# Another table of steps for a transformer block's early x passes, weight sums and h rounds, and two chunks' fold products ahead of the first transposes

## The chip, the cores and the metric

One core of one Trainium2 chip runs the whole program. The metric is device time in microseconds: the median over several executions. Below, TensorE is PE in the profile's rows (PEld its weight loads), VectorE is DVE, ScalarE is ACT, GpSimd is POOL, and SP is the engine that issues most of the DMAs, in order, from one queue.

## The reference

One block of a transformer in float32, 2048 rows of width 1024, 32 heads of 32, and an inner width of 3584:

```python
qkv = layernorm(x) @ wqkv
pq, pk = q @ w_phi, k @ w_phi                    # per head, 32 x 32
phi_q = concat(softmax(pq), softmax(-pq))        # the same for phi_k
kv, z = phi_k^T @ v, sum_s(phi_k)
o = (phi_q @ kv) / (phi_q @ z + 1e-6)
h = x + o @ wo
out = h + relu(layernorm(h) @ w1) @ w2
```

## The kernel before

**Numbers.** Every float32 product is made of three fast ones. Each operand is split in a high part (a copy in the fast format, made by ACT) and a low part (the rest, made by DVE or POOL). `mm3` (lines 181 to 183) issues high x high, high x low and low x high as three matmuls of 128 x 512. Three such matmuls are one *step* of the program; almost all of TensorE's work is a row of steps.

**Items and steps.** The work is a list of items in an order written out by hand: first q, k and v products by tiles of 128 rows ("kv" and "q" items, 8 steps each, item n begins at step 8n), then attention and `wo`, then the two layers of the MLP, up (from step `up0`, 4 steps an item) and down. `when(step, f, ...)` hangs a piece of side work behind a step; the engines' queues are filled in that order and each engine works through its own in order. So the step numbers decide what stands ahead of what on ACT, DVE, POOL and in SP's queue, not when it runs.

**Weights.** `Units` loads weight chunks into six buffers `raw` on SP's queue (lines 376 to 389), ACT (line 124) and DVE or POOL (line 128) split them into ten buffers `w`, at most 10 steps before their use or paced out further ahead.

**Folds.** `w_phi` is multiplied into the weights of k and q first. The first slab (p = 0) does it at the start: `first_fold(k)` makes the products of chunks k and k + 1 from `wt` (line 324), `first_high` (ACT, line 453) and `first_low` (DVE, line 457) split them. The other seven slabs do it at steps during the kv items: `wt_load(p)` on SP (line 320), `fold_part(p)` (line 335 on TensorE), DVE's transposes (line 355), and a store on SP (line 363); the products come back as `raw` chunks. The slabs p = 4 and 5 fold at steps 140 and 172, and their `wt` is requested at steps 120 and 152.

**x.** Tiles 0 to 7 are normalised and turned by TensorE just before use (`X_STEPS`: load, statistics, power, normalisation, two transposes). Tiles 8 to 15 are normalised early and stored to `xnd` in device memory (`X_EARLY`: load, statistics, normalisation; the store of four DMAs follows 4 steps after), and loaded again much later. All loads of x, and two of these reloads, share two buffers `xin`. DVE makes the statistics (line 221), POOL the power (lines 230 to 232), ACT the normalisation (lines 244 and 251).

**Weight sums.** The MLP saves one product in eight by a scheme of seven products in place of eight, for which sums of blocks of w1 and w2 are made: a set is a load of 512 KB `b` (SP, line 410; in the up stage by ACT's queue), four subtractions on POOL (line 420) and a store `t` (SP, line 423). There are 56 sets, placed by the list `places`, 21 of them ("far") during the first kv items.

**h.** Of h's two halves of rows, the second is normalised and turned in four rounds during the up stage of the first half (`turn_pair`, with DVE's transposes at line 876), and each round ends in seven stores `hs` (`turn_store`, line 900). `h_load` (line 916) brings the seven combinations back as `hT`, `h_high` (ACT, line 924) and `h_low` (DVE, line 928) split them.

Of the kernel before, what the change touches and what calls it, by code (L numbers as in the profile page):

```python
# [25 lines left out]
NP = NC // 2  # L26
# [113 lines left out]
def kernel(  # L140
# [25 lines left out]
    def tp_bank():  # L166
        return psum.tile([P, 512], F32, name="tp", bufs=2)
# [20 lines left out]
    def do(n, k, f, *args):  # L188
        at[n, k].append((f, args))
# [21 lines left out]
    def ln_load(key, parts):  # L211
        xin[key] = lnp.tile([P, D], F32, name="xin")
        n = D // len(parts)
        for j, p in enumerate(parts):
            sp.dma_start(xin[key][:, j * n:(j + 1) * n], p)
# [106 lines left out]
    def fold_mm(p, k, ps, sides=(0, 1)):  # L322
        for i in sides:
            pe.matmul(ps[:, i * P:(i + 1) * P], wt_of[p, i][:, k * P:(k + 1) * P],
                      bd[:, i, :], start=True, stop=True)
# [111 lines left out]
    def first_part(k):  # L437

        g, c = k // 2, k % 2
        if g not in first_ps:  # L440
            first_ps[g] = (ac_bank, mm_bank)[g // 2]()
        return first_ps[g][:, 256 * c:256 * (c + 1)]

    def first_place(k):

        key = ("kv", 0, 0, k)
        if key not in W.split:
            W.places[key] = W.ring.take()
            W.split[key] = W.places[key][1]
        return W.split[key]  # L450

    def first_high(k):
        act.activation(first_place(k)[:, 0, 0:256], first_part(k), AF.Copy)
# [8 lines left out]
    def value_low(k, eng):  # L462
        w = first_place(k)
        raw, place = first_raw.pop(k)
        eng.tensor_tensor(out=w[:, 1, 256:512], in0=raw, in1=f32(w[:, 0, 256:512]), op=ALU.subtract)
        place[0] = k % 2 == 1

    def first_fold(k):
        for i in range(2):
            fold_mm(0, k + i, first_part(k + i))  # L470
# [566 lines left out]
    def item(gen, *args, keys):  # L1037
        items.append((gen, args + (keys,)))
        steps.extend((k,) for k in keys)
        return len(items) - 1  # L1040
# [11 lines left out]
    for b, tiles in enumerate(groups):  # L1052
        for hf in range(2):

            pairs = b == 0 and hf == 0
            for j in range(0, 4, 2 if pairs else 1):
# [3 lines left out]
                for half in range(2):  # L1060
                    n = item(wo_pair, tiles[j:j + 2], hf, half, keys=[("wo", hf, 4 * half + k // 2) for k in range(8)])
# [18 lines left out]
    def x_part(t):  # L1080
        return [x[t * P:(t + 1) * P, :]]
# [6 lines left out]
    def when(step, f, *args):  # L1088

        if step < 8 * first_up:  # L1090
            do(step // 8, step % 8, f, *args)
        else:
            do(first_up + (step - 8 * first_up) // 4, step % 4, f, *args)


    X_STEPS = {1: (None, None, None, None, 5, 7), 2: (None, 6, 8, 10, 12, 13), 3: (None, 10, 11, 14, 18, 20),
               4: (9, 19, 20, 24, 27, 28), 5: (15, 25, 26, 29, 35, 38), 6: (25, 33, 35, 37, 41, 44)}
    X_EARLY = ((48, 74, 86), (64, 84, 98), (88, 102, 112), (100, 115, 138), (116, 140, 154), (142, 158, 170),
               (158, 174, 203), (174, 204, 218))
    for t in range(1, NT):  # L1100
        n = t - 1 if t < HT else q_n[1, t - HT] + 1
        turn = 8 * n + 1
# [2 lines left out]
        else:  # L1105

            load_, stats, norm = X_EARLY[t - HT]
            when(load_, ln_load, ("s", t), x_part(t))
# [22 lines left out]
    for p, n in zip(range(1, 8), (3, 9, 13, 17, 21, 25, 29)):  # L1131
        step = 8 * n + (4 if p > 1 else 7)
# [82 lines left out]
    for u in range(32):  # L1215
        start = 8 * (a0 + u) if u >= 8 else 8 * (last_kv + 4) + 19 * u // 2
        slack = 6 if u < 5 else 0
        if u % 2:
            places = (-8 if u < 12 else -1, 6, 10, 13, 16, 19, 25 if u < 16 else 23)
            when(start + 30 + slack, at_num, u - 1)  # L1220
            when(start + 32 + slack, at_low, u - 1)
        elif u < 16:
            places = (-8 if u < 12 else -1, 6, 10, 13, 16, 19, 25)
        else:
            places = (6, 12, 17, 19, 21, 23, 29)
# [28 lines left out]
    up0 = 8 * first_up  # L1254
    for i in range(4):
        for stage in (0, 1, 2, 3, 9, 4, 5, 6, 7, 8):
            when(wo0 + 64 + 40 * i + LN2[i % 2][stage], ln_pair, 0, i, stage)
        for step, *what in TURNS:
            when(up0 + 25 + 84 * i + step, turn_pair, i, *what)
        for j in range(7):  # L1260
            when(wo0 + 64 + 40 * i + LN2[i % 2][10] + j // 2, ln_store, 0, i, j)
            when(up0 + 25 + 84 * i + 56 + j, turn_store, i, j)
    assert wo_n[8, 0] + 10 < first_up

    def up_step(b, p, m):

        return up0 + 4 * (up_n[b, p, m] + 1 - first_up)

    for j, m in enumerate(UP):

        for g in range(2):
            step = up0 + (8 * j + (-62, -32)[g] if j < 4 else 6 * (j - 4) + 10 + 2 * g)
            high = up0 + (8 * j + (-48, -19)[g] if j < 4 else 6 * (j - 4) + 20 + 2 * g)
            when(step, h_load, 0, m, g)
            when(high, h_high, m, g)
            when(high + (2 if j < 4 else 5), h_low, m, g)
            step = up_step(0, NP - 1, m) + 3 * j
            when(step + 3 * g, h_load, 1, m, g)
            when(step + 18 + 4 * g, h_high, m, g)
            when(step + 21 + 4 * g, h_low, m, g)  # L1280
# [8 lines left out]


    sets = [(w, p, j) for w in (1, 2) for p in range(NP) for j in range(2)]
    places = [64 * q + step for q in range(4) for step in (-9, -1, 7, 15, 23, 31) if 64 * q + step > 9]
    far_sets = len(places)
    places += [264, 274, 284, 294, 314, 364, 374]
    slabs = [8 * kv_n[1, q, HT] for q in range(4)]
    places += sorted([slab + step for slab in slabs for step in (8, 20, 32)] + [slab - 3 for slab in slabs[1:3]])
    places += [up0 + 440 + 25 * n for n in range(14)]
    for n, (step, (w, p, j)) in enumerate(zip(places, sets, strict=True)):
        far = n < far_sets
        when(step, t_load, w, p, j, lnp if step > up0 else fp if far and n % 4 > 1 else tsp)  # L1300
# [4 lines left out]
    for b in range(2):  # L1305
        for m in DOWN:
            n = down_n[b, m, NP - 1] + 1
# [50 lines left out]
    x_open(0)  # L1358
    ln_load(("x", 2), x_part(2))
    turned = []  # L1360
    for j in range(2):
        pt = tp_bank().rearrange("p (k n) -> p k n", k=4)
        for k in range(4):
            pe.transpose(pt[:, k, :], xnt["x", 0][:, (4 * j + k) * P:(4 * j + k + 1) * P], ident)
        act.activation(xT[0][:, 0, 4 * j:4 * j + 4, :], pt, AF.Copy)
        turned.append(pt)
# [3 lines left out]
        both = xT[0][:, :, 4 * j:4 * j + 4, :]  # L1370
        v.tensor_sub(both[:, 1], turned[j], f32(both[:, 0]))

    first_fold(0)
    for k in range(2):
        value_high(k, v.tensor_copy)
    for k in range(2):
        value_low(k, pool)
        first_high(k)
    for k in range(2):
        first_low(k)  # L1380
    first_fold(2)
# [90 lines left out]
```

## Time and profile before

| | us |
|---|---|
| median of 3 executions | 1879.9 (1879.06 to 1880.86) |
| the profiled execution | 1880.66 |
| its span, first to last instruction | 1878.9 |
| TensorE busy | 1861.3 |
| VectorE busy | 1074.5 |
| GpSimd busy | 996.0 |
| ScalarE busy | 747.1 |

The mean granted clock of TensorE is 0.998. A row of a timeline gives the start, the duration, the engine, the line, the operation, what it writes and reads, and how often; in brackets stands the idle time before it and what ended that. A matmul's row is longer than its place in the stream, since the next begins before it ends: the distance from one start to the next, 0.227 us when nothing is missing, is what counts.

### The profile page before, as it was taken

To read this page: it belongs to the slowest core of one execution; us is meant where nothing else is said; L and a number is where in the kernel's file an instruction comes from. 1 tells how busy PE (TensorE), PEld (TensorE's weight loads), DVE (VectorE), ACT (ScalarE), POOL (GpSimd) and SP (SyncE) were. 2 spreads that over 40 slices of the span, in tenths; PEclk is the share of its full clock that TensorE was granted. 3 is DMA by queue.
4 is the path that set the end of the run, shared out by engine and by line. 5 is a ranking of instruction groups with operands and counts; after the bars stand their busy time and mean duration, and the time that the engine had idled before them with its cause. 6 is when DMAs were issued, how large, how long until landed. Compare 5 with 4: busy or idle time off the path is not lost.

```text
span 1878.9 us, 31761 instructions
## 1 busy us (share of the span) xinstructions
PE 1861.3 (99%) x11502; PEld 1527.8 (81%) x11502; DVE 1074.5 (57%) x1714; ACT 747.1 (40%) x1272; POOL 996.0 (53%) x956
## 2 busy tenths in 40 slices
PE   9999999999999999999999999999999999999999
PEld 7777888888887888888888878888888888888887
DVE  7877789677889676465554674444433333343333
ACT  5443334222233122355454554444444444444442
POOL 4767756678745888233332334435444444444443
PEclk9999999999999999999999999999999999999999
DMA  6799877445465666898687997877877677767775
GB/s 215 245 308 327 291 243 241 131 149 175 135 224 184 206 213 215 266 292 294 214 286 247 297 316 240 264 249 259 274 237 216 205 227 240 236 215 219 216 214 178
DMA packets 320492, 441.64 MB, mean 235 GB/s; under 512 B 28112, under 2 KB 182736, under 8 KB 320336
## 3 DMA queue, kind: packets, MB, share of 16 engines
q1 hardware_dynamic: 291168, 398.69, 66.4%
q10 hardware_dynamic: 29168, 40.93, 6.6%
q8 instruction: 90, 1.47, 0.3%
q14 instruction: 66, 0.54, 0.1%
HBM read 297.96 MB, written 141.57 MB: 234 GB/s over the span
## 4 chain that ended last, share of the span: by engine, by line
PE 88%; DMA 5%; DVE 2%; SPq 1%; issue 1%; ACT 1%; POOL 1%; DVEq 0%; ACTq 0%; POOLq 0%
PE mm L181 22%; PE mm L182 22%; PE mm L183 22%; PE ac L183 3%; PE ac L182 3%; PE ac L181 3%; PE tp L181 2%; PE tp L183 2%; PE tp L182 2%; DMA hT<-hs 1%; PE tp L720 1%; PE ac L533 1%; PE ac L720 1%; DMA raw<-in_w_dram 1%; PE tp L288 1%
## 5 line engine op out<-in xcount | busy, mean ns | idle before, releaser
L128 POOL TENSOR_TENSOR w<-raw,w 128x512 fp32r<-128x512 f32 x353 | 476.5, 1352 | 641.7 <-ACT w L124 619.6
L124 ACT ACTIVATE w<-raw 128x512 fp32r<-128x512 f32 x686 | 408.9, 626 | 485.0 <-PE mm L183 221.1
L128 DVE TENSOR_TENSOR w<-raw,w 128x512 fp32r<-128x512 f32 x333 | 279.4, 840 | 508.8 <-ACT w L124 503.0
L181 PE MATMUL mm<-w,xT 128*128 128x512 f32 x752 | 298.3, 397 | 2.9 <-ACT w L124 2.9
L182 PE MATMUL mm<-w,xT 128*128 128x512 f32 x752 | 293.4, 390 | 0.5 <-POOL w L128 0.2
L183 PE MATMUL mm<-w,xT 128*128 128x512 f32 x752 | 292.8, 389 | 0.0
L182 PE MATMUL mm<-hT,w 128*128 128x512 f32 x672 | 261.8, 390 | 2.8 <-DVE hT L928 2.8
L181 PE MATMUL mm<-hT,w 128*128 128x512 f32 x672 | 261.6, 389 | 0.7 <-DVE c L954 0.7
L183 PE MATMUL mm<-hT,w 128*128 128x512 f32 x672 | 261.4, 389 | 0.0
L420 POOL TENSOR_TENSOR b<-b 128x256 f32<-128x256 f32 x168 | 133.4, 794 | 78.5 <-DMA b<-in_w_dram 70.0
L181 PEld LDWEIGHTS mm<-w,xT 128*128 128x128 f32 x752 | 141.3, 188 | 35.1 <-ACT w L124 3.3
L182 PEld LDWEIGHTS mm<-w,xT 128*128 128x128 f32 x752 | 141.4, 188 | 31.0 <-POOL w L128 1.1
L183 PEld LDWEIGHTS mm<-w,xT 128*128 128x128 f32 x752 | 141.3, 188 | 29.8
L181 PE MATMUL mm<-w 128*128 128x512 f32 x392 | 152.5, 389 | 0.0
L182 PE MATMUL mm<-w 128*128 128x512 f32 x392 | 152.5, 389 | 0.0
L183 PE MATMUL mm<-w 128*128 128x512 f32 x392 | 152.5, 389 | 0.0
L182 PEld LDWEIGHTS mm<-hT,w 128*128 128x128 f32 x672 | 126.1, 188 | 30.2 <-DVE hT L928 4.1
L181 PEld LDWEIGHTS mm<-hT,w 128*128 128x128 f32 x672 | 126.1, 188 | 27.4 <-DVE c L954 1.1
L183 PEld LDWEIGHTS mm<-hT,w 128*128 128x128 f32 x672 | 126.2, 188 | 25.9
L522 POOL TENSOR_TENSOR zacc<-zacc,kphi 128x512 f32<-128x512 f32 x60 | 82.7, 1378 | 7.0 <-DVE kphi L514 7.0
L181 PEld LDWEIGHTS mm<-w 128*128 128x128 f32 x392 | 73.6, 188 | 15.3
L183 PEld LDWEIGHTS mm<-w 128*128 128x128 f32 x392 | 73.6, 188 | 15.3
(200 smaller groups left out, 3181.0 us busy)
## 6 DMA issues: line engine op xcount, KB each, us to landing
raw<-t SPq DMA_DIRECT2D x224, 256.0 KB, 4.3
raw<-ad SPq DMA_DIRECT2D x196, 256.0 KB, 3.0
raw<-in_w_dram SPq DMA_DIRECT2D x168, 256.0 KB, 3.4
ad<-c SPq DMA_DIRECT2D x112, 256.0 KB, 4.2
b<-in_w_dram SPq DMA_DIRECT2D x42, 512.0 KB, 5.6
t<-b SPq DMA_DIRECT2D x42, 512.0 KB, 3.9
ad<-s SPq DMA_DIRECT2D x84, 256.0 KB, 4.7
ed<-qe ACTq DMA_DIRECT2D x32, 512.0 KB, 4.3
```

The costliest lines, as they stand in the source:

```text
L124: nc.scalar.activation(w[:, 0, :], raw[1], AF.Copy)
L128: eng.tensor_tensor(out=w[:, 1, :], in0=raw[1], in1=w[:, 0, :].bitcast(F32), op=ALU.subtract)
L181: pe.matmul(ps, a_hi, b_hi, start=first, stop=False, skip_group_check=more)
L182: pe.matmul(ps, a_hi, b_lo, start=False, stop=False, skip_group_check=more)
L183: pe.matmul(ps, a_lo, b_hi, start=False, stop=last, skip_group_check=more)
L288: pe.transpose(pt[:, k, :], xn[:, (4 * j + k) * P:(4 * j + k + 1) * P], ident)
L420: pool.tensor_tensor(out=tsum[j, *out], in0=tsum[j, *a], in1=tsum[j, *b], op=ALU.subtract)
L522: pool.tensor_tensor(out=zacc[s], in0=zacc[s], in1=phi_of[key], op=ALU.add)
L533: pe.matmul(kv_ps[s][g][32 * i:32 * (i + 1), 0:64], vt[:, 32 * h:32 * (h + 1)], phi[:, 64 * h:64 * (h + 1)], start=first, stop=last)
L720: pe.matmul(banks[g][32 * c:32 * (c + 1), r * P:(r + 1) * P], kvL[rows, 4 * q + 2 * sd + h // 4, 32 * (h % 4):32 * (h % 4 + 1)], phT[rows, ...
```

## The change

It has five parts. The products of fold chunks 0 and 1 and their high parts are placed ahead of the transposes of the first x tile. Tile 6's statistics, power and normalisation go 3, 2 and 1 steps earlier. The passes of x tiles 12 to 15 go from load steps 116, 142, 158, 174 to 140, 168, 206, 232, with their statistics 14 steps after each. Of the far sets of weight sums two, at steps 119 and 183, are taken out, and the up stage gets 16 sets at a pace of 22 steps in place of 14 at 25. Of h's rounds, the second half's turns come every 80 steps and not 84; the loads of its combinations are planned up to 3 steps earlier; and the low halves of the first half's last three combinations 2 steps earlier.

```diff
-    X_STEPS = {... 6: (25, 33, 35, 37, 41, 44)}
-    X_EARLY = (... (100, 115, 138), (116, 140, 154), (142, 158, 170),
-               (158, 174, 203), (174, 204, 218))
+    X_STEPS = {... 6: (25, 30, 33, 36, 41, 44)}
+    X_EARLY = (... (100, 115, 138), (140, 154, 166), (168, 182, 203),
+               (206, 220, 230), (232, 246, 268))
...
-            when(up0 + 25 + 84 * i + step, turn_pair, i, *what)
+            when(up0 + 25 + 80 * i + step, turn_pair, i, *what)
...
-            when(up0 + 25 + 84 * i + 56 + j, turn_store, i, j)
+            when(up0 + 25 + 80 * i + 56 + j, turn_store, i, j)
...
-            when(high + (2 if j < 4 else 5), h_low, m, g)
-            step = up_step(0, NP - 1, m) + 3 * j
+            when(high + (2 if j < 4 else 3), h_low, m, g)
+            step = up_step(0, NP - 1, m) + 5 * j // 2
             when(step + 3 * g, h_load, 1, m, g)
...
-    places = [64 * q + step for q in range(4) for step in (-9, -1, 7, 15, 23, 31) if 64 * q + step > 9]
+    places = [64 * q + step for q in range(4) for step in (-9, -1, 7, 15, 23, 31) if 64 * q + step not in (-9, -1, 7, 119, 183)]
...
-    places += [up0 + 440 + 25 * n for n in range(14)]
+    places += [up0 + 440 + 22 * n for n in range(16)]
...
     turned = []
+    first_fold(0)
+    for k in range(2):
+        first_high(k)
     for j in range(2):
         pt = tp_bank().rearrange("p (k n) -> p k n", k=4)
...
-    first_fold(0)
     for k in range(2):
         value_high(k, v.tensor_copy)
     for k in range(2):
         value_low(k, pool)
-        first_high(k)
```

On TensorE, at the start (`ones` is a warm-up, `ident,xn` the transposes of x tile 0, `bd,wt` the fold products, `w,xT` the first projection), old rows with - and new ones with +:

```order
 L1345 MATMUL tp<-ones 128x128 x11
-L1364 MATMUL tp<-ident,xn 128x128 x8
-L324 MATMUL ac<-bd,wt 128x128 x8
+L324 MATMUL ac<-bd,wt 128x128 x4
+L1367 MATMUL tp<-ident,xn 128x128 x8
+L324 MATMUL ac<-bd,wt 128x128 x4
 L583 MATMUL mm<-w,xT 128x512 x4
 L324 MATMUL mm<-bd,wt 128x128 x8
```

Four of the eight products (two rows each in the profile) stand ahead of the transposes now, and four behind.

In SP's queue, near step 116 (`raw<-wpk` and `raw<-in_wv` are halves of one weight chunk, `xnd<-xn` the store of an early x tile, `xin` the load of tile 12, `b` a set's load, `wt` and `wpk<-wp` a fold's weights and result), before:

```order
L376 DMA raw<-wpk_76 128x256
L377 DMA raw<-in_wv_dram 128x256
L258 DMA xnd_102<-xn 32x4x256 x4
L215 DMA xin<-in_x_dram 128x1024
L376 DMA raw<-wpk_76 128x256
L377 DMA raw<-in_wv_dram 128x256
L410 DMA b<-in_w_dram 128x4x256
L320 DMA wt<-in_wqkT_dram 128x1024 x2
L363 DMA wpk_77<-wp 128x4x256 x2
```

and now:

```order
L376 DMA raw<-wpk_76 128x256
L377 DMA raw<-in_wv_dram 128x256
L258 DMA xnd_102<-xn 32x4x256 x4
L376 DMA raw<-wpk_76 128x256
L377 DMA raw<-in_wv_dram 128x256
L320 DMA wt<-in_wqkT_dram 128x1024 x2
L363 DMA wpk_77<-wp 128x4x256 x2
```

Tile 12's load and one set's load have left this place; the slab's last chunk follows the store directly.

On VectorE, at the begin of the up stage (`w<-raw` a weight split, `hT7` the two low halves of one combination, `c` a sum of two banks), before:

```order
L128 TENSOR_TENSOR w_9528<-raw_9383,w_9528 128x512
L128 TENSOR_TENSOR w_9572<-raw_9427,w_9572 128x512
L128 TENSOR_TENSOR w_9618<-raw_9469,w_9618 128x512
L928 TENSOR_TENSOR hT7_9488<-hT7_9488 128x4x256 x2
L954 TENSOR_TENSOR c110_9515<-ac_9623,c110_9515 128x512
```

and now:

```order
L128 TENSOR_TENSOR w_9514<-raw_9369,w_9514 128x512
L128 TENSOR_TENSOR w_9558<-raw_9413,w_9558 128x512
L928 TENSOR_TENSOR hT7_9474<-hT7_9474 128x4x256
L128 TENSOR_TENSOR w_9605<-raw_9455,w_9605 128x512
L928 TENSOR_TENSOR hT7_9474<-hT7_9474 128x4x256
L954 TENSOR_TENSOR c110_9501<-ac_9610,c110_9501 128x512
```

One low half has moved ahead of the third weight split.

More of the change, by code (lines that the diff above doesn't have):

```diff
@@ L1096 @@
     X_STEPS = {1: (None, None, None, None, 5, 7), 2: (None, 6, 8, 10, 12, 13), 3: (None, 10, 11, 14, 18, 20),
-               4: (9, 19, 20, 24, 27, 28), 5: (15, 25, 26, 29, 35, 38), 6: (25, 33, 35, 37, 41, 44)}
-    X_EARLY = ((48, 74, 86), (64, 84, 98), (88, 102, 112), (100, 115, 138), (116, 140, 154), (142, 158, 170),
-               (158, 174, 203), (174, 204, 218))
+               4: (9, 19, 20, 24, 27, 28), 5: (15, 25, 26, 29, 35, 38), 6: (25, 30, 33, 36, 41, 44)}
+    X_EARLY = ((48, 74, 86), (64, 84, 98), (88, 102, 112), (100, 115, 138), (140, 154, 166), (168, 182, 203),
+               (206, 220, 230), (232, 246, 268))
     for t in range(1, NT):
```

## The prediction, made before the changed kernel ran

> **What bounds the kernel now.** I read the page's busy table first, then TensorE's list of waits, then its busy time in stretches of 20 us, and last the instructions around each hole.
>
> ```profile
> span 1878.9 us, 31761 instructions
> PE 1861.3 (99%) x11502; PEld 1527.8 (81%) x11502; DVE 1074.5 (57%) x1714; ACT 747.1 (40%) x1272; POOL 996.0 (53%) x956
> ```
>
> TensorE is the bound: it idles 17.6 us in all. The change moves work and removes none from TensorE, so it can only win holes in TensorE's stream, or open new ones. Where the holes are (waits of PE; then stretch, length, PE busy, granted clock, DMA share, GB/s):
>
> ```profile
> PE mm L181 <- ACT w L124: 2.9, 1, 2.9
> PE mm L182 <- DVE hT L928: 2.8, 3, 1.3
> PE tp L335 <- DMA wt<-in_wqkT_dram: 2.5, 2, 2.3
> ...
> 120.00:140.00 20.00, 16.89 (x190) 1.00 0.96 303
> 140.00:160.00 20.00, 17.46 (x158) 0.96 0.99 324
> 160.00:180.00 20.00, 19.72 (x126) 0.95 0.93 317
> 1060.00:1080.00 20.00, 19.33 (x85) 1.00 1.05 341
> 1100.00:1120.00 20.00, 17.88 (x78) 1.00 0.91 286
> ```
>
> Every large hole lies in a stretch where the DMA engines are full (0.91 to 1.05). There the queue on SP runs late, and TensorE waits for a weight chunk, a fold's weights or a piece of h. All three edits of the step tables touch these stretches. One program step is three matmuls, 0.68 us at the steady 0.227 us from one start to the next.
>
> **The change part by part.**
>
> *a. Fold products first.* The start, in order:
>
> ```profile
> 7.80 1.47 PE L1364 MATMUL tp<-ident,xn 128*128 128x128 f32 x8 [1.91 <-ACT xn L238]
> 8.15 0.49 DVE L460 CAST w<-raw 128x256 fp32r<-128x256 f32 x2 [0.67 <-DMA raw<-in_wv_dram]
> 9.06 3.25 PE L324 MATMUL ac<-bd,wt 128*128 128x128 f32 x16
> 12.07 1.17 PE L583 MATMUL mm<-w,xT 128*128 128x512 f32 x4
> ...
> 8.37:11.78 3.41, 3.41 (x18) 3.41 (x17) 0.35 (x3) 1.96 (x5) 1.41 (x2) 0.50 1.07 373
> ```
>
> The 16 products run from 9.06 to about 12.0 because the granted clock is 0.50 between 8.37 and 11.78. Half of them (8 rows) now stand before the transposes. Their weights `wt` are issued on SP just ahead of the `raw` chunk that lands by 8.15, so 8.15 is their latest; I put them at about 7.5; 8 rows at full clock are 8 x 0.107 = 0.85 us, so the transposes start near 8.3 instead of 7.8. The transposes then run at half clock, then 8 products x 0.213 = 1.7 us, and the first projection starts near 11.4 instead of 12.07. Some of its four matmuls still fall into the slow window. I take -0.5 us; ends: +0.4 (weights only at 8.15, nothing regained) and -2.0 (no slow window).
>
> The Trainium skill, page "TensorE: Matmul & The Clock Gate", Part 1, says that the clock is set by a free-running window of about 3.4 us and halves after an idle one. The trace agrees in length (0.50 for 3.41 us); by that rule real matmuls ahead of 8.37 could keep the next window at full rate, which is rival 2.
>
> *b. Statistics of x tile 6 at step 30.*
>
> ```profile
> 41.99 1.44 DVE L355 STREAM_TRANSPOSE wp<-mm 128x256 f32<-128x256 f32 x4
> 45.98 1.27 DVE L221 BATCH_NORM_STATS2 st<-xin 128x6 f32<-128x512 f32 x2
> 50.30 0.66 PE L288 MATMUL tp<-ident,xn 128*128 128x128 f32 x4 [0.40 <-ACT xn L244]
> ```
>
> They now stand before the eight `wp` transposes and not behind them. The normalisation then waits for the Exp ahead of it on ACT instead, which comes 1.3 us later (near 47.5 to 48.1); normalised by 49.4, the tile is there when TensorE comes at 49.74. The hole at 50.30 (start to start 0.79 against 0.23) closes: -0.55; ends -0.55 and +1.0 (DVE's kv work is now 1.3 us later).
>
> *c. Early x passes and two weight-sum sets out of the crowd.* The first large hole, as PE's rows, the chain that ended there, and SP's queue:
>
> ```profile
> 122.19 0.39 PE L183 MATMUL mm<-w,xT 128*128 128x512 f32 x1
> 125.47 0.50 PE L181 MATMUL mm<-w,xT 128*128 128x512 f32 x1 [2.88 <-ACT w L124]
> 126.19 0.50 PE L182 MATMUL mm<-w,xT 128*128 128x512 f32 x1 [0.22 <-DVE w L128]
> ...
> 119.55 5.14 DMA raw<-in_wv_dram
> ...
> 118.58 0.39 SPq L215 DMA_DIRECT2D xin<-in_x_dram  x1
> ...
> DMA to landing us min/median/max: 2.3/3.5/6.4
> ```
>
> The hole is 3.05 + 0.50 = 3.55 us. The last chunk of `raw` was issued right behind tile 12's 512 KB load and took 5.14 us. That load goes (step 116 to 140). The chunk is issued about 0.3 us sooner and should land in 2.3 to 3.5 us: 1.9 to 3.1 us sooner. I take -2.5; ends -1.0 and -3.5.
>
> The second hole is fold 5 (step 172) against fold 4 (step 140):
>
> ```profile
> 129.99 0.39 PE L183 MATMUL mm<-w,xT 128*128 128x512 f32 x1
> 132.77 0.50 PE L181 MATMUL mm<-w,xT 128*128 128x512 f32 x1
> ...
> 154.43 0.39 PE L183 MATMUL mm<-w,xT 128*128 128x512 f32 x1
> 157.16 0.41 PE L335 MATMUL tp<-wt,wphi 32*32 32x256 f32 x2 [2.34 <-DMA wt<-in_wqkT_dram]
> 161.20 0.80 PE L181 MATMUL mm<-w,xT 128*128 128x512 f32 x1
> ...
> 149.75 0.98 SPq L320 DMA_DIRECT2D wt<-in_wqkT_dram  x2
> SPq L423 <- POOL b L420: 17.0, 8, 4.7
> DMA packets 18136, 20.57 MB, mean 316 GB/s; under 512 B 1205, under 2 KB 17106, under 8 KB 18130
> ```
>
> One passage takes 2.78 us, the other 6.77: 3.99 lost, 2.5 of it idle and the rest mostly the half clock after it. `wt` was planned 20 steps ahead of this fold, so at 154.4 - 13.6 = 140.8, and issued at 149.75. Ahead of it now go tile 12's load and the set of step 119 (its load, its store, and four POOL sums; SP waited 17.0 us for such sums): three times 0.52 MB, which at 316 GB/s is 5.0 us. Tile 12's new load takes the place of tile 13's old one, so that is even. TensorE itself arrives 0.5 + 0.55 + 2.5 = 3.55 us sooner, so of 3.55 + 2.5 us needed 5.0 are there: 1.1 us stay. -2.9; ends 0 and -4.0. The idle in 160 to 180 (0.28 us) should go as well: -0.3, ends 0 and -0.6.
>
> What moves lands in 125 to 235 us: loads of tiles 13, 14, 15 at steps 168, 206, 232 with their stores (four DMAs each) and POOL scales. Each load now has 14 steps, 9.5 us, until DVE wants it. Landing alone takes 6.3 us here, and DVE already lost 1.7 us to one such load:
>
> ```profile
> xin<-in_x_dram SPq DMA_DIRECT2D x4, 512.0 KB, 6.3
>   DVE st L221: 1.7, 1
> ```
>
> DVE's kv steps and half the weight splits queue behind it. Also, the reload of tile 9 (step 257) now shares a buffer with tile 15, whose normalisation stands at step 268, so SP stops some 9 us there. Behind it are chunks wanted at step 320, 50 steps later, and a set whose sums then hold POOL; I find nobody who needs POOL sooner, so nothing. For new waits of DVE and for the two sets that now come in the up stage (16 at a pace of 22 steps, 14 at 25 before) I put +1.0; ends 0 and +5.
>
> *d. h's rounds.* First the low halves at `high + 3`, then the turns of the second half at a pace of 80:
>
> ```profile
> 822.21 1.06 ACT L924 ACTIVATE hT<-hT 128x1024 fp32r<-128x1024 f32 x1 [2.02 <-DMA hT<-hs]
> 824.43 2.35 DVE L928 TENSOR_TENSOR hT<-hT 128x1024 fp32r<-128x1024 f32 x2
> 826.84 0.50 PE L182 MATMUL mm<-hT,w 128*128 128x512 f32 x1 [0.70 <-DVE hT L928]
> ...
> 1040.83 0.90 SPq L900 DMA_DIRECT2D hs<-s  x2
> 1052.47 0.67 SPq L916 DMA_DIRECT2D hT<-hs  x1
> 1096.78 0.97 SPq L916 DMA_DIRECT2D hT<-hs  x2
> ```
>
> At 824.43 DVE did both halves of `hT7` back to back behind a weight split. One of them now stands ahead of that split, so the second ends 1.2 us sooner and TensorE's hole of 0.86 closes: -0.8; ends 0 and -0.9.
>
> The rows of 1060 to 1080 and 1100 to 1120 above lack 0.67 + 2.12 = 2.8 us of PE, in three holes; with the restart after each (some 0.16 us, as at 826.84 in the rows above: 0.86 lost, 0.70 of it wait) that is 3.3 us. The last turn's seven stores move 12 steps, 8.2 us, to where the DMA engines have room, and take 1.84 MB, some 5 us of DMA, out of the crowd ahead of the h loads. These loads are planned up to 3 steps (2 us) sooner too. Each hole is shorter than 1.5 us, so far less than this gain would do. -2.8; ends 0 and -3.3.
>
> *Sum:* -0.5 - 0.55 - 2.5 - 2.9 - 0.3 + 1.0 - 0.8 - 2.8 = -9.35 us. The profiled execution took 1880.66 us, 1.8 around its span, and 0.8 over the median of 1879.9. It gives 1871.3 against itself and **1870.5** against the median.
>
> **The rivals.**
> 1. *Half of it.* TensorE comes sooner, but DMA-bound queues do not follow: fold 5 and the second h round keep their holes (2.9 + 2.8 back). For it: DMA share 0.99 and 1.05, and TensorE's own gain of 3.55 already eats most of the 5.0. Against: bytes do leave both stretches. 1876.2.
> 2. *The slow clock at the start goes too.* Then the first projection starts near 10.0, and a. is -2.0 instead of -0.5: 1869. Against: only some 0.9 us of matmuls are added to that window, of 3.4 us.
> 3. *Slower: DVE stops for the late x tiles.* DVE stops by SP's lateness + 6.3 - 9.5 us. Splits are made up to 10 steps (6.8 us) ahead, so TensorE stops only when SP is over 10 us late. The `wt` above was 9 us late. Were SP 13 us late at each of the four loads, TensorE would lose 3 us at each, 12 us, and c. would win nothing: 1879.9 + 12 - 0.5 - 0.55 - 0.8 - 2.8, about 1887.
> 4. *Holes only move.* The stretch 175 to 240, which has no hole now, gets some 1 MB more. If fold 6 and fold 7 wait there as fold 5 did, c. is given back: about 1877 to 1880.
>
> **How the numbers follow.** The forecast has 0.62, rival 1 0.16, rival 2 0.08, rival 3 0.05, rival 4 0.09. About 0.2%, 3.8 us, is what a measurement can tell from no change; the line is at 1876.1. Faster: 0.62 + 0.08 + half of rival 1 + a little of rival 4, and I allow a few hundredths for its forecast going short: 0.80. Same: 0.14. Slower: 0.06. The range is 1865.5, where every hole is won (about -14), to 1877, where rival 1 ends and rival 4 begins.
>
> **What would show it.** Right: the first projection near 11.4; no wait of PE at fold 5 over 1.2 us and a granted clock of 1.00 in 140 to 180; 120 to 140 with PE above 19; no PE wait for `hT` above 0.3. Wrong: PE waits for `w` splits between 140 and 240, DVE waiting for `xin` more than 3 us at a time, or 1060 to 1120 still short of 3 us of PE.

## The result, and the profile after

| | median us | executions | ratio to before, 95% interval |
|---|---|---|---|
| before | 1880.86 | 5 (1879.06 to 1883.91) | |
| changed | 1866.3 | 5 (1865.42 to 1869.39) | 0.9924 (0.9911 to 0.9938) |

The change takes 14.6 us, some 0.8%; the forecast was 1870.5, its range 1865.5 to 1877. The profiled execution took 1866.3 us with a span of 1864.5, against 1880.66 and 1878.9. The page's busy table and TensorE's whole list of waits, after the change:

```profile
span 1864.5 us, 31755 instructions
PE 1856.4 (100%) x11502; PEld 1526.2 (82%) x11502; DVE 1067.1 (57%) x1714; ACT 748.3 (40%) x1272; POOL 993.0 (53%) x956
...
PE tp L1345 <- POOL ones L1341: 1.6, 1, 1.6
PE tp L335 <- DMA wt<-in_wqkT_dram: 1.4, 2, 1.1
PE tp L288 <- DVE wp L355: 0.6, 1, 0.6
PE ac L324 <- DMA wt<-in_wqkT_dram: 0.3, 1, 0.3
PE tp L720 <- issue: 0.3, 1, 0.3
```

TensorE idles 8.1 us instead of 17.6. All waits for `w` and for `hT` are gone from this execution; what is left at fold 5 is 1.4 us, and there are two new waits, 0.6 us for VectorE's transposes `wp` and 0.3 us for the weights of the fold products at the start. In stretches of 20 us (PE busy, granted clock, DMA share), to set beside those of before:

```profile
120.00:140.00 20.00, 20.00 (x206) 15.98 (x205) 14.27 (x37) 7.41 (x12) 9.78 (x12) 1.00 0.92 286
140.00:160.00 20.00, 18.63 (x199) 14.57 (x198) 12.47 (x33) 5.23 (x8) 13.78 (x19) 1.00 0.98 343
160.00:180.00 20.00, 20.00 (x206) 16.03 (x205) 16.79 (x36) 9.46 (x16) 14.89 (x15) 1.00 0.91 297
1060.00:1080.00 20.00, 20.00 (x90) 16.57 (x89) 17.22 (x18) 14.01 (x21) 6.19 (x4) 1.00 1.03 338
1100.00:1120.00 20.00, 20.00 (x90) 16.57 (x89) 10.32 (x11) 8.42 (x15) 11.58 (x11) 1.00 0.85 289
```

TensorE is full in four of the five, though in three of these four the DMA engines are nearly as full as before (0.02 to 0.04 less). The start, TensorE's rows:

```profile
1.56 4.75 PE L1345 MATMUL tp<-ones 128*128 128x128 f32 x22 [1.56 <-POOL ones L1341]
6.14 0.39 PE L324 MATMUL ac<-bd,wt 128*128 128x128 f32 x2
6.88 0.94 PE L324 MATMUL ac<-bd,wt 128*128 128x128 f32 x6 [0.35 <-DMA wt<-in_wqkT_dram]
7.81 1.09 PE L1367 MATMUL tp<-ident,xn 128*128 128x128 f32 x8
8.74 1.06 PE L324 MATMUL ac<-bd,wt 128*128 128x128 f32 x8
9.55 1.17 PE L583 MATMUL mm<-w,xT 128*128 128x512 f32 x4
```

The last of the weights come at 6.9, the transposes are not delayed, no row behind the warm-up runs at half clock, and the first projection starts at 9.55 instead of 12.07.

Where the 14.4 us between the two profiled executions came from is seen by setting the same matmul of line 182 beside itself in the two traces (there are 2576 in each). After minus before, at these places in the time of before:

| at, us | 30 | 60 | 118 | 128 | 190 | 800 | 840 | 1120 | 1800 |
|---|---|---|---|---|---|---|---|---|---|
| shift, us | -2.55 | -2.29 | -2.61 | -6.32 | -9.88 | -9.77 | -10.68 | -14.37 | -14.37 |

So the start gave 2.55; tile 6 took 0.26, and 0.32 came back by 118; the hole at 122 gave 3.7, fold 5 with what follows 3.56, the low half of `hT7` 0.9 and the second h round 3.7. Between 190 and 800 us hardly anything is lost (0.11).

### The profile page after: what moved, and what is told of

It reads as the page before. It is cut to its first block, busy times and chain, and to the rows that moved or that the text cites. A ratio compares the mean times of both kernels' runs of the same rounds, so it can differ in the third digit from the quotient of the medians.

```text
span 1864.5 us, 31755 instructions
## 1 busy us (share of the span) xinstructions
PE 1856.4 (100%) x11502; PEld 1526.2 (82%) x11502; DVE 1067.1 (57%) x1714; ACT 748.3 (40%) x1272; POOL 993.0 (53%) x956
## 4 chain that ended last, share of the span: by engine, by line
PE 95%; DMA 2%; DVE 1%; SPq 1%; ACT 0%; POOL 0%; issue 0%; DVEq 0%; POOLq 0%
PE mm L181 24%; PE mm L183 24%; PE mm L182 24%; PE ac L183 4%; PE ac L181 4%; PE ac L182 4%; PE tp L183 2%; PE tp L181 2%; PE tp L182 2%; DMA wt<-in_wqkT_dram 1%; PE tp L720 1%; DMA b<-in_w_dram 1%; PE ac L533 1%; PE ac L720 1%; PE tp L288 1%; DMA wpk<-wp 0%
## 5 line engine op out<-in xcount | busy, mean ns | idle before, releaser
L420 POOL TENSOR_TENSOR b<-b 128x256 f32<-128x256 f32 x160 | 125.6, 785 | 74.2 <-DMA b<-in_w_dram 66.4
```

What stands on the lines that cost most here:

```text
L420: pool.tensor_tensor(out=tsum[j, *out], in0=tsum[j, *a], in1=tsum[j, *b], op=ALU.subtract)
```

## The experiments

Twelve kernels ran, each with four to eleven executions and a profile, in three groups; each group shared a chip and its runs of before. An interval is about 0.0013 each way, 2.4 us, so two variants of the changed kernel 2 us apart can't be told by their times. For them the profile's holes carry the verdict.

| kernel | median us | ratio to before, 95% interval |
|---|---|---|
| 1: before, fold products first | 1878.3 | 0.9987 (0.9976 to 0.9998) |
| 2: before, x passes and sums | 1873.68 | 0.9958 (0.9945 to 0.9970) |
| 3: before, h's rounds | 1876.19 | 0.9971 (0.9960 to 0.9983) |
| 4: changed, tile 6 back | 1868.06 | 0.9931 (0.9919 to 0.9944) |
| 5: changed, old start | 1867.56 | 0.9932 (0.9920 to 0.9945) |
| 6: the same, longer warm-up | 1867.68 | 0.9934 (0.9921 to 0.9946) |
| 7: changed, x passes back | 1869.27 | 0.9941 (0.9927 to 0.9954) |
| 8: changed, sums back | 1869.64 | 0.9941 (0.9928 to 0.9953) |
| 9: changed, pace 84 back | 1868.07 | 0.9941 (0.9929 to 0.9954) |
| 10: changed, h loads back | 1866.12 | 0.9925 (0.9912 to 0.9939) |
| 11: changed and three more moves | 1864.69 | 0.9917 (0.9903 to 0.9930) |
| 12: changed, again | 1866.67 | 0.9926 (0.9913 to 0.9940) |

The medians of before were 1880.42 beside 1 to 4, 1880.83 beside 5 to 8, and 1879.49 beside 9 to 12. One execution of kernel 10 took 3786 us; nothing in the others is like it, and the median hardly depends on it.

The second table is worked out from the profiles: in each stretch, how much later than 0.227 us (0.15 for the short ones) a matmul starts after the one before it, summed over those that are 0.16 us or more late. Times are of each kernel's own span.

| us lost in | 62 to 76 | 116 to 132 | 146 to 159 (fold 5) | 161 to 182 | 800 to 860 | 1040 to 1115 |
|---|---|---|---|---|---|---|
| before | 0.2 | 3.5 | 2.9 | 1.0 | 0.9 | 3.3 |
| changed | 0 | 0 | 1.8 | 0 | 0 | 0 |
| 12, the same again | 0 | 1.2 | 1.3 | 0.6 | 0.7 | 0 |
| 1 fold first | 0.6 | 4.8 | 3.1 | 2.0 | 0 | 4.6 |
| 2 x and sums | 0.8 | 0.9 | 1.2 | 0 | 0.8 | 2.8 |
| 3 h's rounds | 1.0 | 3.9 | 0.7 | 2.7 | 0 | 0 |
| 4 tile 6 back | 1.1 | 2.5 | 0 | 0 | 0 | 0 |
| 5 old start | 0 | 1.1 | 0.5 | 0 | 0 | 0 |
| 6 longer warm-up | 0 | 1.1 | 3.7 | 0 | 0 | 0 |
| 7 x back | 0 | 2.4 | 0 | 2.5 | 0 | 0 |
| 8 sums back | 0 | 1.4 | 4.0 | 0 | 0 | 0 |
| 9 pace back | 0 | 0.9 | 1.4 | 0.2 | 0 | 1.6 |
| 10 h loads back | 0 | 1.0 | 0.3 | 0 | 0 | 0 |
| 11 three more moves | 0 | 0 | 0 | 1.2 | 0 | 0 |

### The three large parts alone (1, 2, 3)

Each is the kernel before with only these lines of the diff:

```diff
1: +    first_fold(0)          (ahead of the transposes, with first_high)
2: X_EARLY of tiles 12 to 15; places without 119 and 183, 22 * n for n in range(16)
3: 80 * i for 84 * i; high + 3 for high + 5; 5 * j // 2 for 3 * j
```

> The kernel before with one part of the change alone: the products of fold chunks 0 and 1 and their high parts ahead of the first tile's transposes. The prediction (half the clock from 8.4 to 11.8 us stays): -0.5 us, the first projection near 11.4 us. Rival, from the trace after (the slow window goes, first projection at 9.55 there): -2.5 us, the first projection near 9.6, granted clock 1.00 in the first 20 us, and nothing given back later, so about 1878.3 against 1880.8. A third way: the 2.5 us are won at the start but the queues on SP do not follow, and the holes near 122 and 154 us grow by as much: within 0.5 us of before.

> The kernel before with the early x passes of tiles 12 to 15 moved and the two sets of weight sums taken out (16 in the up stage). The prediction: -2.5 - 2.9 - 0.3 + 1.0 = -4.7 us, 1.1 us of wait for wt at fold 5, and some waits of VectorE or in the up stage. Theory from the trace after: the hole at 122 goes whole (-4.0 with what follows) and fold 5 gives -3.2 to -4.0; no new wait: -7.2 to -8.0 us. If the wait that is left at fold 5 in the trace after (1.4 us) is what TensorE's own gain at the start (2.5 us) ran into, it is gone here, since TensorE comes 2.5 us later: -8.0. If it is the queue alone, it stays: -7.2.

> The kernel before with h's rounds alone at their new steps. The prediction: -0.8 - 2.8 = -3.6 us. From the trace after: all four holes (826, 1069, 1101, 1108 us) gone, 0.86 + 0.83 + 1.45 + 0.99 = 4.1 and 0.1 us of restart at each: -4.1 to -4.5 us. Rival (the two sets that are still at steps 119 and 183 here, and only 14 in the up stage, make no difference to it): if the up stage's sets mattered, one of the three later holes would come back or the gain be another than in the whole change.

The parts lower the ratio by 0.0013, 0.0042 and 0.0029 (2.4, 7.9 and 5.5 us; 2.1, 6.7 and 4.2 by the medians), together 0.0084; the whole by 0.0076 and 0.0074 in its two measurements. That is additive within the intervals.

Kernel 1 won 2.57 us at the start (first projection at 9.50, no window at 0.50). But its profiled execution took 1880.8 us: at 190 us the same matmul stood 0.01 us later than in before, since the holes at 120 and 175 were larger. That looks like the third way that was expected, but kernel 3, which has the same passes and sums and won nothing at the start, loses 3.9 and 2.7 us at these places in its profile. So whether TensorE's gain turned into waiting there is not shown. Over eleven executions the gain is 2.4 us (0.4 to 4.5 by the interval): most of what was won at the start was kept.

Kernel 2 has both holes, small (PE's rows):

```profile
122.34 0.51 PE L181 MATMUL mm<-w,xT 128*128 128x512 f32 x1 [0.26 <-ACT w L124]
...
152.21 0.40 PE L335 MATMUL tp<-wt,wphi 32*32 32x256 f32 x2 [0.56 <-DMA wt<-in_wqkT_dram]
```

The wait at fold 5 is 0.9 us in all, and it is 0.9 us in kernel 12, which has the new start: nothing says that what is left there is what TensorE's gain at the start ran into. Its three holes for `hT` are those of before (2.8 us lost, against 3.3). Kernel 3 has none of them: h's part is apart from the rest. Kernel 3's median is 4.2 us under before's, near what its four holes say (4.1).

### What halves the clock at the start (5, 6)

```diff
5: the changed kernel with first_fold(0) and first_high behind the transposes, as before
6: the same, and
-    for _ in range(11):
+    for _ in range(14):
```

> The changed kernel with the start as before: all eight fold products behind the transposes. Theory 1, a clock window that runs freely and halves the clock after a window with about 1.9 us of matmuls in 3.41 (TensorE stands from 6.3 to 7.7 us here): by where a window happens to end, the first projection comes at 10.3 us (clock 1.00) or near 12.0 (clock 0.50 for 3.41 us), in different executions of the same kernel; the time is 0.8 or 2.5 us over the changed kernel's, 1 to 2 us in the median. Theory 2, the order itself sets the slow window: the first projection near 12 in every profile with this start, and +2.5 us.

> The same with 14 warm-up products in place of 11, so that TensorE is busy until about 7.5 us. Theory 1 (it is the gap in TensorE's work that halves the clock): clock 1.00 in the first 20 us, the first projection at 10.3, and 0.8 us over the changed kernel. Theory 2 (the order sets it): 0.50 for 3.41 us and the first projection near 12, +2.5 us.

Four profiles have the old start with the short warm-up: before and kernels 2, 3 and 5. The warm-up and the first projection of kernels 3 (half clock), 2 (full clock; kernel 5 has the same, at 10.37) and 12 (the new start), two rows each, in this order:

```profile
1.56 4.10 PE L1345 MATMUL tp<-ones 128*128 128x128 f32 x22 [1.56 <-POOL ones L1341]
12.05 0.48 PE L583 MATMUL mm<-w,xT 128*128 128x512 f32 x1
```
```profile
1.56 4.99 PE L1345 MATMUL tp<-ones 128*128 128x128 f32 x22 [1.56 <-POOL ones L1341]
10.29 0.48 PE L583 MATMUL mm<-w,xT 128*128 128x512 f32 x1
```
```profile
1.56 4.09 PE L1345 MATMUL tp<-ones 128*128 128x128 f32 x22 [1.56 <-POOL ones L1341]
9.57 1.17 PE L583 MATMUL mm<-w,xT 128*128 128x512 f32 x4
```

The same code with the old start gives 12.05 or 10.3, and the warm-up's own length tells which. Its rows stand 0.213 us apart, which is half clock, until the first full window, and 0.111 us from there on, and that window begins at another moment in each execution. Where it begins early (4.96 in before, 4.47 in kernel 3), the warm-up is over at 5.7 to 5.9, TensorE stands for 1.9 to 2.1 us inside one window, and the next runs at half clock. Where it begins at 6.3 (kernels 2 and 5), the stand is 1.1 to 1.2 us and nothing follows. Kernels 7, 10 and 12 have the new start with windows as early as these (4.89, 4.44 and 4.47): the first projection is at 9.54, 9.76 and 9.57 all the same, since products fill part of the stand (in kernel 12, 2.38 us of that window are busy, in kernel 3 1.30). Theory 2 is wrong by kernels 2 and 5, and theory 1 holds, with 1.3 to 1.5 us of busy time in the window that halves the clock where it said 1.9. Kernel 6, with the longer warm-up, has its first projection at 10.29, but decides nothing: its window began at 5.86, and with the short warm-up some 2 us of it would have been busy too (an estimate from the rows above), more than in any window here that was followed by half clock.

The order is worth 0.8 us at the first projection and 1.1 to 1.2 us by 30 us, where kernels 2, 5 and 6 stand 1.3 to 1.4 us ahead of before and the changed kernel and kernel 12 2.5. The slow window costs 1.3 us more in before and 1.7 to 1.8 in kernel 3, and it came in two of the four profiles with the old start and its short warm-up. The times of 5 and 6 (1.3 and 1.4 us over the first median of the changed kernel) are of that size, but not resolved by themselves.

### x passes or sums (7, 8)

```diff
7: the changed kernel with X_EARLY as before, the sets of sums as changed
8: the changed kernel with places as before, X_EARLY as changed
```

> The changed kernel with the passes of tiles 12 to 15 back at 116, 142, 158, 174; the sets of sums stay out. Theory (tile 12's load of 512 KB ahead of the slab's last chunk makes the hole at 122): that hole is back with 2.5 to 3.5 us, and fold 5 waits 1.5 to 3.5 us since tile 12's load and those of tile 13 are ahead of its wt: +4 to +6 us. Rival (the sums make both holes): the same as the changed kernel within 1 us.

> The changed kernel with the sets of sums back at steps 119 and 183 and 14 in the up stage at a pace of 25; the x passes stay moved. Theory (the set at 119 stands behind the slab's last chunk, so it leaves the hole at 122 alone but delays fold 5's wt by its load and store): the hole at 122 under 1 us, fold 5 waits 1.5 to 3 us more than the 1.4 of the changed kernel, +1.5 to +3 us. Rival (the sums count for nothing): within 1 us of the changed kernel.

PE's rows of kernel 7, then of kernel 8:

```profile
121.65 0.50 PE L181 MATMUL mm<-w,xT 128*128 128x512 f32 x1 [1.70 <-ACT w L124]
171.81 0.50 PE L182 MATMUL mm<-w,xT 128*128 128x512 f32 x1 [1.72 <-POOL w L128]
```
```profile
152.25 0.41 PE L335 MATMUL tp<-wt,wphi 32*32 32x256 f32 x2 [2.37 <-DMA wt<-in_wqkT_dram]
```

With the x passes back, 2.4 us are lost near 120 and 2.5 at 172 in a wait for POOL; fold 5 doesn't wait at all. With the sums back, fold 5 loses 4.0 us and the hole near 120 1.4, more than the 1 us expected. By themselves these sizes settle little: with both edits in place kernel 4 loses 2.5 us near 120 and kernel 6 3.7 at fold 5, and with neither kernel 3 loses 0.7 at fold 5.

For tile 12's load the landing of the slab's last chunk settles it. The chunk that ended the hole, issue and time to landing, in kernel 7 and then in kernel 4, the longest without that load:

```profile
115.20 5.66 DMA raw<-in_wv_dram
```
```profile
117.57 4.62 DMA raw<-in_wv_dram
```

In the four profiles with tile 12's load directly ahead (before, 1, 3, 7) the two halves of this chunk landed 4.8 to 5.7 us after their issue, in the ten without it after 3.0 to 4.6. What differs besides, from one execution to the next, is how late SP comes to it: 117.4 to 119.6 us, in the time of before.

For the set at step 119 nothing of the kind separates the runs. The four profiles that have it (before, 1, 3, 8) lose 0.7 to 4.0 us at fold 5, 2.7 in the mean, the nine with its place empty (the eight with both edits, and 7) 0 to 3.7, 1.1 in the mean: likely, not shown. My expectation for kernel 7, a wait at fold 5 too, was wrong, and its 3.0 us over the changed kernel's first median are less than the 4 to 6 expected. Kernel 8 is 3.3 us over it. Both are at the edge of what the intervals tell.

### Tile 6 (4)

```diff
-  6: (25, 30, 33, 36, 41, 44)
+  6: (25, 33, 35, 37, 41, 44)
```

> The changed kernel with tile 6's statistics, power and normalisation back at steps 33, 35, 37. The prediction (that part is worth -0.55): 0.55 us slower than the changed kernel, a hole of 0.56 us near 47 us. Rival, from the trace after (a hole of 0.80 us at 42 us where TensorE waits for VectorE's transposes behind the statistics): the two holes trade places and it is 0.1 to 0.3 us faster than the changed kernel, so the part is worth nothing. Either is near what a run can tell; the place of the hole decides.

The hole of 0.56 us is back near 47 and that of 0.80 at 42 is gone, so those two trade places. Rows of the changed kernel on VectorE and TensorE:

```profile
40.71 1.44 DVE L355 STREAM_TRANSPOSE wp<-mm 128x256 f32<-128x256 f32 x4
42.08 1.40 DVE L355 STREAM_TRANSPOSE wp<-tp 128x256 f32<-128x256 f32 x4
...
42.96 0.63 PE L288 MATMUL tp<-ident,xn 128*128 128x128 f32 x4 [0.64 <-DVE wp L355]
```

Yet kernel 4 isn't faster. It loses 1.1 us more near 70, in what looks like a chain over four engines. Rows of kernel 4 (POOL's power of tile 6, SP's store of the sums, the next slab's first chunk, TensorE), then of the changed kernel:

```profile
45.08 0.22 POOL L230 TENSOR_SCALAR sc<-mv 128x1 f32<-128x1 f32 x1 [2.44 <-DVE mv L224]
49.98 0.53 SPq L423 DMA_DIRECT2D t<-b  x1
56.31 0.58 SPq L376 DMA_DIRECT2D raw<-wpk  x1
69.30 0.50 PE L182 MATMUL mm<-w,xT 128*128 128x512 f32 x1 [0.40 <-POOL w L128]
```
```profile
47.24 0.53 SPq L423 DMA_DIRECT2D t<-b  x1
53.62 1.16 SPq L376 DMA_DIRECT2D raw<-wpk  x1
```

With late statistics POOL stands 2.44 us at the power, ahead of the four sums of a set; SP stands at that set's store; the slab's first chunk is asked for 2.7 us later. All five profiles with the old steps lose 0.2 to 1.1 us in 62 to 76, none of the nine with the new steps does. So the hole near 70 goes with the old steps. The chain is read from these two profiles; what lies between the chunk and the wait at 69 was not tested by itself.

### h's pace or loads (9, 10)

```diff
9:  the changed kernel with 84 * i in place of 80 * i
10: the changed kernel with 3 * j in place of 5 * j // 2
```

> The changed kernel with the turns of h's second half back at a pace of 84 steps. Theory (the last turn's seven stores, 12 steps later again, fill the DMA engines ahead of the loads of h): holes for hT between 1050 and 1100 us are back with 2 us or more, +2 to +3.3 us. Rival (the loads' earlier steps alone made the gain): no wait for hT over 0.3 us, within 0.5 us of the changed kernel.

> The changed kernel with the loads of the second half's combinations back at 3 j steps. Theory (the pace of the turns made the gain): no hole for hT over 0.5 us, within 0.5 us of the changed kernel. Rival (the loads' steps made it): the three holes between 1050 and 1100 us are back, +2 to +3.3 us.

Kernel 10 has no wait for `hT` at all, so with the new pace the loads' steps are worth nothing that can be seen. In kernel 9 two are back (its PE rows):

```profile
1079.55 0.50 PE L182 MATMUL ac<-hT,w 128*128 128x512 f32 x1 [0.64 <-DVE hT L928]
1096.83 0.50 PE L182 MATMUL mm<-hT,w 128*128 128x512 f32 x1 [0.65 <-DVE hT L928]
```

They lose 1.6 us, less than the 2 expected and not the 3.3 of before. The pace carries the gain: all ten profiles with it lose nothing between 1040 and 1115 us, the four without it 1.6 to 4.6. That the earlier loads save half when the pace is missing rests on kernel 9's one profile.

### Three more moves, and the changed kernel again (11, 12)

```diff
+        fold_turn(p, (0, 1) if p == 1 else (2, 3))      # then the other two
-    ... (88, 102, 112), ...
+    ... (88, 102, 118), ...
+        do(18 if p == 5 else max(n - 2, 1), 0, wt_load, p, sp)
```

> The changed kernel with three more moves, one for each hole that is left: VectorE transposes the banks that the transposes of x want first in fold 1 (the hole of 0.80 us at 42 us goes; if another bank is wanted as soon, it only moves), the normalisation of x tile 10 goes from step 112 to 118, so that its store of four DMAs stands behind the slab's last chunk (that chunk is issued 2 us sooner; the hole near 121, 0 to 2.5 us in the runs, goes), and the weights of fold 5 are asked for at step 144, not 152 (issued some 5 us sooner; the wait at fold 5, 0 to 3.3 us in the runs, goes). All three: -2 to -4 us against the changed kernel, and less spread. Rival (these holes only move to the next chunk, as the DMA engines are full there): within 1 us.

> The changed kernel once more, on the same chip and in the same call as the one with three more moves: 1866.3 again, within 1.5 us. Theory: the holes of the first profile are not all there is; near 121 us and at fold 5 each execution has its own wait, 0 to 2.5 and 0 to 3.3 us. Rival: the holes are the same to 0.3 us in each profile, 0 and 1.4 us.

TensorE's waits in kernel 11 (whole list), then three of kernel 12:

```profile
PE tp L1345 <- POOL ones L1341: 1.6, 1, 1.6
PE mm L182 <- POOL w L128: 0.8, 1, 0.8
PE ac L324 <- DMA wt<-in_wqkT_dram: 0.2, 1, 0.2
```
```profile
PE tp L335 <- DMA wt<-in_wqkT_dram: 0.9, 2, 0.7
...
PE mm L181 <- ACT w L124: 0.6, 1, 0.6
PE mm L182 <- DVE hT L928: 0.5, 1, 0.5
```

All three holes are gone in kernel 11's profile, and 1.2 us are lost instead in a wait for POOL's split at 166. Its four executions took 1862.92 to 1865.53 us, those of kernel 12 1864.3 to 1868.71. It is 2.0 us under kernel 12 in the median, but the intervals overlap: probably better, not shown. Kernel 12 answers its own question: the loss near 121 is 0 in one profile and 1.2 us in the other of the same kernel, that at fold 5 1.8 and 1.3.

## Why the prediction was right, point by point

**The bound and the places.** TensorE was the bound, and the gain is the idle time that the prediction listed, with the slow window at the start. No engine became a new bound. The size was partly luck: the forecast was 4.2 us too slow, its larger terms were too small, and the measured median lies 0.8 us from the fast end of the range, which stood for every hole won. Of the four signs of being right three came: a clock of 1.00 and no wait over 1.2 us at fold 5 (1.1 and 0.3, so only just), PE above 19 in 120 to 140, and no wait for `hT`. The first projection was at 9.55 and not 11.4.

**a, -0.5: mis-sized.** The two profiles give -2.5, the medians -2.1 (alone) and -1.3 (undone). The step that failed is "the transposes then run at half clock": I took the half window of one execution for a fixed part of the start. Rival 2 had the mechanism and got 0.08; my argument against it, that only 0.9 us of matmuls are added, was wrong, since before stood so near the border (1.50 us busy, see the last section) that this is plenty. The weights came at 6.9 and not 7.5, and a row at full clock takes 0.111 us and not 0.107; neither matters. The Trainium skill's page "TensorE: Matmul & The Clock Gate", Part 1, had the decisive word, "free-running": by it the window's place differs between executions, as 12.05 and 10.3 with the same code show here.

**b, -0.55: the size about right, the reason not.** The hole at 50.30 closed as forecast, but I looked only at ACT's Exp behind the statistics and missed that TensorE's next transposes want the banks that the delayed `wp` empties. 0.26 us were lost there by 60 us. The gain came near 70, where the five profiles with the old steps lose 0.7 us in the mean and those with the new steps nothing; it seems to come by POOL and SP, a chain that I had not followed: POOL's power was listed among the moved steps, but not what queues behind it.

**c, -5.7 and +1.0 for new waits: -6.7 in the median, -7.9 by the ratio.** c1 was said -2.5 for a hole of 3.55. In eight profiles with both edits (changed, 2, 4, 5, 6, 9, 10, 12) 0 to 2.5 us stay, 1.1 in the mean, against 3.7 in the four with tile 12's load, so 2.6: right, and by the mechanism that it named, though of this some 1.4 us are a shorter landing (5.3 against 3.9 us for the second halves), less than the 1.9 to 3.1 said, and the rest an earlier issue and the clock. c2 left 1.1 us at fold 5; the same eight leave 0 to 3.7, 1.3 in the mean: right in size, but how much of it is due to the set and how much to tile 12's load, which it counted both, stays open. The mis-sized term is the +1.0, which was put for waits that cost TensorE nothing. VectorE's waits for x in the profile after:

```profile
DVE st L221 <- DMA xin<-in_x_dram: 5.6, 2, 2.8
```

One of the two is the first tile's at 4 us, as long before the change; the other, 2.8 us at 139 us, is tile 12's. In kernels 6 and 8 this second one was 4.2 and 3.2 us, over the 3 us that I had named as a sign of being wrong, and TensorE had no wait there even so: the sign was badly chosen. Between 190 and 800 us TensorE loses only 0.1 us more than before. Nor do the 16 sets in the up stage cost anything: from 860 to 1860 us the changed kernel's profile loses nothing.

**d, -3.6: -4.2 alone, -5.5 by the ratio.** All four holes closed in kernel 3. I gave the loads' earlier steps a share; kernel 10 shows that the pace does it without them. The low half ahead of a weight split isn't as safe as one profile says: kernel 12 lost 0.7 us there again, and kernel 1, with the old steps, nothing.

**The rivals.** "Half of it" and "holes only move" were wrong for the whole. Of the slower rival only the first step was seen: VectorE stops for a late tile, TensorE doesn't. The time of "holes only move" does not follow from its words: giving back all of c makes 1875.2 us; 1877 to 1880 needs two new holes of the size of fold 5's.

Against its own profile the sum was 5.0 us short (-9.35 for -14.37): 2.0 in a, 1.0 in the new waits, 1.6 in c's holes, which happened to close whole or nearly so there, and 1.0 in d; b was 0.5 too much.

## What to carry to other kernels

Where a queue of DMAs runs late, look at what stands directly ahead of the late request and move that: without tile 12's load ahead of it the chunk landed 1.4 us sooner in the mean, and TensorE got no new wait for it. A hole's length in one profile is a draw (0 to 2.5 us and 0 to 3.7 us at two places here): profile the same kernel more than once before a term of that size is put down to it. And when work is moved, follow every engine's queue: a 0.2 us instruction on POOL that waits for another engine stood ahead of sums, a store and a weight chunk, and all three came later.

## What the runs showed of the hardware

The clock's border is sharp, by the busy time that the profile gives. Windows of 3.41 us, by the granted clock's own edges, for before, kernel 3, kernel 8 and kernel 6 (PE busy is the second figure after the window, the clock the third from the end):

```profile
4.96:8.37 3.41, 1.50 (x13) 1.31 (x13) 1.30 (x5) 0.94 (x2) 1.09 (x3) 1.00 1.03 328
121.00:124.41 3.41, 1.58 (x7) 0.96 (x6) 0.00 (x0) 0.00 (x0) 1.77 (x2) 1.00 0.88 296
124.41:127.82 3.41, 2.13 (x8) 1.53 (x9) 2.02 (x5) 1.16 (x3) 1.47 (x2) 1.00 1.02 354
```
```profile
123.94:127.35 3.41, 1.33 (x5) 0.81 (x5) 1.47 (x4) 0.90 (x2) 0.73 (x1) 1.00 1.03 360
127.35:130.76 3.41, 3.41 (x10) 2.62 (x9) 2.51 (x7) 2.11 (x3) 2.46 (x5) 0.50 1.06 390
```
```profile
150.08:153.49 3.41, 0.95 (x32) 0.50 (x32) 0.73 (x3) 1.12 (x2) 3.17 (x5) 1.00 0.98 319
153.49:156.90 3.41, 3.21 (x97) 2.23 (x98) 0.39 (x2) 0.00 (x0) 1.57 (x2) 0.50 1.09 382
```
```profile
149.21:152.62 3.41, 1.63 (x8) 1.01 (x6) 2.81 (x7) 2.84 (x3) 3.23 (x5) 1.00 0.97 275
152.62:156.04 3.42, 1.90 (x84) 1.03 (x88) 0.14 (x1) 0.63 (x1) 3.19 (x6) 1.00 1.04 387
```

TensorE's row behind the gap in kernel 6:

```profile
153.96 0.41 PE L335 MATMUL tp<-wt,wphi 32*32 32x256 f32 x2 [3.12 <-DMA wt<-in_wqkT_dram]
```

In the first 185 us of the 14 profiles, each of the seven windows with 0.6 to 1.50 us of busy PE was followed by one at 0.50, and each of the seven with 1.58 to 1.95 by one at 1.00. So what counts in these runs is not the length of a gap but how much of it falls into one window: the gap of 1.91 us at before's start halved the clock, one of 2.88 us in before at 122 and one of 3.12 us in kernel 6, each shared between two windows, did not. The Trainium skill's page "TensorE: Matmul & The Clock Gate", "Why this matters for your kernels", advises against gaps over some 3 us; here these measurements go the other way.

A small load behind a large one on SP's queue lands late. Near 60 us, where a load of x of 512 KB stands between chunks in every profile, the two half chunks (128 KB each) directly ahead of it landed 2.6 to 3.9 us after their issue and the two directly behind it after 4.1 to 5.8 (one of the 28 ahead has no landing on record).
